# Moving 49 rows between DMA engines: seven of 128 stores written by 14 of the 16 engines

## The chip, the cores and the metric

The kernel runs on one core of one Trainium2 chip. The metric is the device time of the whole program in microseconds; lower is better. A profile comes from one execution; its span, from the first to the last instruction, is about 1.8 us shorter than that execution's time.

## The reference

It is the forward and backward pass of attention with one query per head: 64 heads (2 x 32), 8192 keys, head size 128, bf16.

```python
def _fwd_reference(q, k, v):
    scale = q.shape[-1] ** -0.5
    scores = jnp.einsum("bhqd,bhkd->bhqk", q, k) * scale
    p = _softmax(scores, axis=-1)
    return jnp.einsum("bhqk,bhkd->bhqd", p, v)
# ...
    _out, _vjp = jax.vjp(_f, q, k, v)      # returned: out, dq, dk, dv
    _grads = _vjp(grad_out)
```

For each head, k and v (2 MB each) are read once, and dk and dv (2 MB each) are written once. That is 268 MB in and 268 MB out. The small outputs are out and dq.

## The kernel before

Each 2 MB array of a head lies in SBUF as 128 partitions of one 16 KB row each. A row is 64 consecutive keys. There are 12 such tiles ("slots"). A load fills a slot, the engines compute, the gradient is written over the input in the same slot, and the slot is stored from there. So a new load has to wait for the store of the slot that it takes.

```python
NTILE = 12
# ...
    load_eng = nc.sync        # loads: hardware queue
    store_eng = nc.gpsimd     # stores: GpSimd's software queue
# ...
    def slot_of(i, w):
        n = 2 * i + w
        return n if n < NTILE else slot_of(i - NTILE // 2, 1 - w)

    def load(i, w, pieces=(NCH,)):
        h = heads[i]
        t = kvp.tile([P, NT, D], BF16, tag=f"kv{slot_of(i, w)}", name="kvt")
        h.tile[w] = t
        src = (v_v if w else k_v)[i]
        # ... (one transfer of 128 partitions x 16 KB, except for head 0)
            pin(load_eng.dma_start(out=t[:, n0:n1, :], in_=src[:, n0:n1, :]))
# ...
    qd_nat = evp.tile([P, CH, P], BF16, tag="ev", name="qd_nat")
    for w, a in enumerate((q, grad_out)):
        pin(load_eng.dma_start(out=qd_nat[:BH, w, :], in_=a.rearrange("b h s d -> (b h s) d")))
# ...
    def outer(i, w, c, ends):
        # ... VectorE writes the gradient over h.tile[w] ...
        if c + 1 in ends:
            at = ends.index(c + 1)
            b0, b1 = (ends[at - 1] if at else 0) * CH, (c + 1) * CH
            dst = (dv_v if w else dk_v)[i]
            pin(store_eng.dma_start(out=dst[:, b0:b1, :], in_=h.tile[w][:, b0:b1, :]))
```

For every head but the last, `ends` is one value, so that the store is one transfer of 2 MB. The last head is stored in eight transfers of 512 KB.

Of the kernel before, what the change touches and what calls it, by code (L numbers as in the profile page):

```python
# [16 lines left out]
CW = 64  # L17
NG = 2
NTILE = 12

@with_exitstack
def kernel(
# [12 lines left out]
    B, H, Sq, D = q.shape  # L36
    Sk = k.shape[2]
    P = nc.NUM_PARTITIONS
    assert Sq == 1 and D == P
    BH = B * H  # L40
    assert BH <= P
    NT = Sk // P
# [5 lines left out]
    load_eng = nc.sync  # L48
    store_eng = nc.gpsimd
    pin = tc.keep_in_program_order  # L50
# [25 lines left out]
    def slot_of(i, w):  # L76

        n = 2 * i + w
        return n if n < NTILE else slot_of(i - NTILE // 2, 1 - w)

    def load(i, w, pieces=(NCH,)):
        h = heads[i]
        t = kvp.tile([P, NT, D], BF16, tag=f"kv{slot_of(i, w)}", name="kvt")
        h.tile[w] = t
        src = (v_v if w else k_v)[i]
        c = 0
        for m in pieces:
            n0, n1 = c * CH, (c + m) * CH
            pin(load_eng.dma_start(out=t[:, n0:n1, :], in_=src[:, n0:n1, :]))  # L89
            c += m  # L90

    load(0, 0, (1, 1, 2))

    qd_nat = evp.tile([P, CH, P], BF16, tag="ev", name="qd_nat")
    for w, a in enumerate((q, grad_out)):
        pin(load_eng.dma_start(out=qd_nat[:BH, w, :], in_=a.rearrange("b h s d -> (b h s) d")))  # L96

    load(0, 1)
    for j in range(1, min(NTILE // 2, BH)):
        load(j, 0)  # L100
        load(j, 1)
# [268 lines left out]
    def outer(i, w, c, ends):  # L370

        h = heads[i]
        n0 = c * CH
        shape = [P, CH, D // 2, 2]
        pin(
            nc.vector.tensor_tensor(  # L376
                out=h.tile[w][:, n0 : n0 + CH, :].rearrange("p n (e t) -> p n e t", t=2),
                in0=h.qb[w][:]
                .rearrange("p (e t) -> p e t", t=2)
                .unsqueeze(1)  # L380
                .to_broadcast(shape),
                in1=h.pair[w][:, n0 : n0 + CH, :].unsqueeze(2).to_broadcast(shape),
                op=ALU.mult,
            )
        )
        if c + 1 in ends:
            at = ends.index(c + 1)
            b0, b1 = (ends[at - 1] if at else 0) * CH, (c + 1) * CH
            dst = (dv_v if w else dk_v)[i]
            pin(store_eng.dma_start(out=dst[:, b0:b1, :], in_=h.tile[w][:, b0:b1, :]))  # L390

    A1 = NCH + 4
    O1 = A1 + 1
# [3 lines left out]
    last = list(range(1, NCH + 1))  # L397
    AHEAD = NTILE // 2

    prev = None  # L400
    for g in range(SL * BH + O0 + NCH + 4 - SL):
# [15 lines left out]
        if x := within(O1):  # L417
            outer(x[0], 1, x[1], last if x[0] == BH - 1 else whole)
        if x := within(O0):
            outer(x[0], 0, x[1], last if x[0] == BH - 1 else whole)  # L420
        ev = None
        if g < SL * BH:
            i, r = divmod(g, SL)
# [74 lines left out]
```

## Time and profile before

| kernel before | |
|---|---|
| time, median of 4 runs | 1304.37 us (1304.22 to 1304.51) |
| span of the profiled run | 1303.1 us |
| TensorE busy | 89% |
| DMA | 9 tenths or more busy in 38 of 40 slices, mean 414 GB/s |
| last v load: its 15th completion / its 16th | 1243.0 / 1264.9 us |
| last store: issued / 15th completion / 16th | 1291.6 / 1295.1 / 1301.1 us |

The kernel is limited by DMA. These lines are from the profile page of the kernel before. The line DMA cuts the span into 40 slices and gives the mean busy share of the 16 DMA engines in tenths. The line GB/s gives what they moved in each slice.

```profile
span 1303.1 us, 42566 instructions
...
DMA  9999999999999999999999999999999999999965
GB/s 390 423 427 427 427 427 427 428 426 430 427 427 427 427 427 429 427 428 427 429 427 427 429 427 424 418 420 425 421 416 420 419 421 421 418 421 422 394 281 206
```

What to see is a plateau of 427 GB/s. From the 25th slice on it drops to about 420, and in the last two slices DMA is about half idle. The next lines are from the same page: the queues (packets, MB, share of 16 engines' time) and the transfers (count, size, median us from issue to landing).

```profile
q1 hardware_dynamic: 19040, 268.51, 48.9%
q0 software_dynamic: 19296, 268.44, 48.7%
q8 instruction: 150, 2.46, 0.7%
...
out_dram<-kvt POOLq DMA_DIRECT2D x126, 2048.0 KB, 40.4
kvt<-in_v_dram SPq DMA_DIRECT2D x64, 2048.0 KB, 49.3
kvt<-in_k_dram SPq DMA_DIRECT2D x63, 2048.0 KB, 49.4
```

Loads wait for stores, and TensorE waits only a little for loads. These are two answers on the waits of the kernel before, the load queue's own and TensorE's. The columns are: who waits, for what, total us, times, longest us.

```profile
SPq L89 <- DMA out_dram<-kvt: 1140.6, 116, 24.2
...
PE tp L166 <- DMA kvt<-in_v_dram: 91.1, 54, 2.3
PE tp L166 <- DMA kvt<-in_k_dram: 17.7, 21, 1.3
```

The mean over 16 engines hides the cause. The trace of the kernel before holds 4288 completions for 268 transfers, 16 for each, and a transfer has landed with the last of them. One engine gives one of the 16: after the 15th of the last store only one engine of sixteen still moves data (0.06, below). Here they are for three stores of the kernel before, sorted, in us after the issue:

```text
issued at  616.0: 15.6 15.7 15.7 16.0 16.1 17.9 22.6 27.6 27.9 28.0 28.0 28.2 28.4 28.5 29.3 42.0
issued at 1021.8: 12.7 12.7 13.1 13.8 13.8 14.4 14.8 18.0 19.9 19.9 19.9 19.9 20.2 20.3 20.6 42.0
issued at 1183.6: seven at 12.7 to 13.6, eight at 16.4 to 18.8, one at 41.9
```

One engine is 13, then 21, then 23 us behind the next slowest. All others get ahead of it and then run short of work, because each slot waits for that engine (the load queue waits 1140.6 us for stores, above). The end of the kernel shows this directly. This is the answer that sums stretches of time (us of each engine's busy time and instruction count, granted clock, DMA share, GB/s), kernel before:

```profile
core 0: us, PE busy (x) PEld busy (x) DVE busy (x) ACT busy (x) POOL busy (x), PEclk, DMA share, GB/s
1205.00:1230.00 25.00, 23.16 (x373) 17.09 (x371) 16.79 (x39) 18.24 (x12) 1.06 (x2) 0.88 1.00 422
1252.00:1256.00 4.00, 3.97 (x74) 3.29 (x76) 2.70 (x9) 3.34 (x5) 0.00 (x0) 1.00 0.08 29
1295.50:1300.50 5.00, 0.00 (x0) 0.00 (x0) 0.00 (x0) 0.00 (x0) 0.00 (x0) 0.50 0.06 26
```

A DMA share of 0.06 is one engine of sixteen (1/16 = 0.0625), and 26 GB/s is what this one engine moved. From 1252 to 1256 us one engine is almost alone (0.08), because it still owes its rows of the last loads. From 1295.5 to 1300.5 us it is alone with its rows of the last stores.

The packet records of the trace can be strung into 16 chains, one for each engine, by matching each packet's end with the next one's start. In the kernel before, most 16 KB rows took exactly 611 ns; a few took much longer, so that the mean is 615 to 620 ns in nearly every chain. In one chain it is 636 ns, and there many rows lie on steps of about 9 ns (618, 627, 636, 646 and so on). The chains carry no numbers. The 150 instruction packets fall on eight other chains, 17 to 20 each; five chains have none, and two more have most of the packets of another small instruction queue (31 in all). One of the 150 took about 0.98 us and the packet after it about 1.0 us, so roughly 1.4 us more work for each (an estimate: 0.98 + 1.0 less the 0.611 of a usual row). These chains are a reconstruction from start and end times; the records do not name engines. A second reconstruction gave the same slow chain and the same eight, but it exchanged chains in the last 100 us; so the ends and idle times of single engines rest on one reconstruction.

### The profile page before, as it was taken

How to read it: one execution, taken by the hardware profiler on the slowest of the kernel's cores; microseconds unless marked ns; L12 is line 12 of the kernel's file. 1: busy time of each engine (PE TensorE's matmuls, PEld its weight loads, DVE VectorE, ACT ScalarE, POOL GpSimd, SP SyncE). 2: the span in 40 equal slices, each digit the busy share in tenths (PEclk: the TensorE clock that was granted, in tenths of full speed). 3: DMA queues.
4: the chain of work that ended last, by engine and by line, in shares of the span. 5: the costliest groups of instructions: out<-in, count | busy, mean ns of one | idle time of the engine just before them, and what ended most of it. 6: DMA issues, size and time to landing. Idle time of an engine off the chain costs nothing.

```text
span 1303.1 us, 42566 instructions
## 1 busy us (share of the span) xinstructions
PE 1154.0 (89%) x19268; PEld 873.0 (67%) x19268; DVE 937.5 (72%) x2122; ACT 974.8 (75%) x641; POOL 72.4 (6%) x142
## 2 busy tenths in 40 slices
PE   6999998889898888988989888989898898888984
PEld 5777776667676666666766666667676676666662
DVE  2888887677776777767777677676776767777776
ACT  6888887777787777777778777777777777777771
POOL 0000000000000000000000000000000000000001
PEclk9999999899898999989989999898898989999986
DMA  9999999999999999999999999999999999999965
GB/s 390 423 427 427 427 427 427 428 426 430 427 427 427 427 427 429 427 428 427 429 427 427 429 427 424 418 420 425 421 416 420 419 421 421 418 421 422 394 281 206
DMA packets 38517, 539.67 MB, mean 414 GB/s; under 512 B 4544, under 2 KB 4544, under 8 KB 5824
## 3 DMA queue, kind: packets, MB, share of 16 engines
q1 hardware_dynamic: 19040, 268.51, 48.9%
q0 software_dynamic: 19296, 268.44, 48.7%
q8 instruction: 150, 2.46, 0.7%
q14 instruction: 31, 0.25, 0.0%
HBM read 268.47 MB, written 268.47 MB: 412 GB/s over the span
## 4 chain that ended last, share of the span: by engine, by line
issue 80%; DMA 11%; POOL 4%; DVE 2%; PE 1%; POOLq 0%; SPq 0%; DVEq 0%
DMA kvt<-in_v_dram 8%; POOL out_dram L390 4%; DMA out_dram<-kvt 3%; DVE kvt L376 1%; PE tp L166 1%; POOLq L390 0%; PE acc L321 0%; DVE sel L344 0%; PE dpw L177 0%; SPq L89 0%; SPq L96 0%; DVE sel L338 0%; PE sw L177 0%; PE acc L358 0%; DVE pair L252 0%
## 5 line engine op out<-in xcount | busy, mean ns | idle before, releaser
L168 ACT COPY ev<-tp 128x2048 bf16<-128x2048 bf16 x512 | 954.0, 1865 | 300.3 <-PE tp L166 290.6
L166 PE MATMUL tp<-ident_bf,kvt 128*128 128x128 bf16 x8192 | 573.4, 226 | 108.9 <-DMA kvt<-in_v_dram 91.1
L376 DVE TENSOR_TENSOR kvt<-qb,pair 128x2048 bf16<-128x2048 bf16 x512 | 621.1, 1214 | 0.2
L166 PEld LDWEIGHTS <-kvt 128*128 128x128 bf16 x8192 | 501.4, 102 | 116.2 <-DMA kvt<-in_v_dram 95.8
L177 PEld LDWEIGHTS <-ev 128*128 128x128 bf16 x8192 | 242.8, 96 | 211.2 <-issue 164.4
L321 PE MATMUL acc<-kvt,dS_pad 128*64 128x512 bf16 x1024 | 177.2, 430 | 1.3 <-DVE dqT L361 1.3
L321 PE MATMUL acc<-kvt,E_pad 128*64 128x512 bf16 x1024 | 159.8, 392 | 0.0
L177 PE MATMUL dpw<-qdT,ev 128*128 128x1 bf16 x4096 | 140.9, 164 | 12.0 <-DVE qb L159 10.7
L189 DVE TENSOR_REDUCE mp<-sw 128x1 f32<-128x64 f32 x64 | 14.3, 224 | 186.5 <-PE sw L177 186.5
L344 DVE SCALAR_TENSOR_TENSOR sel<-acc,diag,sel 128x128 f32<-128x128 f32 x384 | 134.6, 351 | 13.6
L177 PE MATMUL sw<-qdT,ev 128*128 128x1 bf16 x4096 | 142.5, 164 | 1.1 <-ACT ev L168 1.1
L390 POOL DMA_DIRECT2D out_dram<-kvt x134 | 71.3, 532 | 1219.2 <-DVE kvt L376 1186.8
L321 PEld LDWEIGHTS <-dS_pad 128*64 128x64 bf16 x1024 | 38.5, 113 | 26.9 <-issue 9.4
L229 DVE CAST E_pad<-E_f 128x64 bf16<-128x64 f32 x64 | 12.5, 195 | 60.6 <-ACT E_f L220 60.6
L321 PEld LDWEIGHTS <-E_pad 128*64 128x64 bf16 x1024 | 36.3, 108 | 21.0 <-issue 0.2
L358 PE MATMUL acc<-ones,sel 128*128 128x1 f32 x256 | 43.3, 239 | 6.2 <-DVE sel L344 6.2
L264 PE MATMUL dpw<-ld,ones 128*128 128x1 f32 x256 | 46.3, 250 | 0.1
L338 DVE TENSOR_SCALAR sel<-acc,diag 128x128 f32<-128x128 f32 x128 | 44.0, 344 | 0.0
L358 PEld LDWEIGHTS acc<-ones,sel 128*128 128x128 f32 x256 | 39.0, 193 | 7.3 <-DVE sel L344 7.3
L235 DVE CUSTOM_DVE_ANT_0 junk<-E_f,dpw 128x64 bf16<-128x64 f32 x64 | 14.1, 220 | 40.2 <-PE dpw L177 40.2
L159 DVE CAST qb<-dpw 128x128 bf16<-128x128 f32 x128 | 35.4, 277 | 6.0 <-PE dpw L150 6.0
L264 PEld LDWEIGHTS dpw<-ld,ones 128*128 128x128 f32 x256 | 38.2, 188 | 0.5 <-DVE ld L235 0.5
(42 smaller groups left out, 303.2 us busy)
## 6 DMA issues: line engine op xcount, KB each, us to landing
out_dram<-kvt POOLq DMA_DIRECT2D x126, 2048.0 KB, 40.4
kvt<-in_v_dram SPq DMA_DIRECT2D x64, 2048.0 KB, 49.3
kvt<-in_k_dram SPq DMA_DIRECT2D x63, 2048.0 KB, 49.4
out_dram<-kvt POOLq DMA_DIRECT2D x8, 512.0 KB, 11.3
kvt<-in_k_dram SPq DMA_DIRECT2D x2, 512.0 KB, 4.5
kvt<-in_k_dram SPq DMA_DIRECT2D x1, 1024.0 KB, 7.1
out_dram<-nat SPq DMA_DIRECT2D x2, 16.0 KB, 5.0
qd_nat<-in_q_dram SPq DMA_DIRECT2D x1, 16.0 KB, 6.8
```

Of the source, the lines that this page charges most:

```text
L159: pin(nc.vector.tensor_copy(out=h.qb[w][:], in_=h.qbp))
L166: pin(nc.tensor.transpose(tp[:, t, :], src[:, c * CH + t, :], ident_bf[:]))
L168: pin(nc.scalar.copy(out=ev[:], in_=tp[:]))
L177: nc.tensor.matmul(dst[:, c * CH + t : c * CH + t + 1], lhsT=ev[:, t, :], rhs=qdT[:, w, i : i + 1], start=True, stop=True,)
L189: pin(nc.vector.reduce_max(out=h.mp[:], in_=h.s, axis=AX.X))
L264: nc.tensor.matmul(out, lhsT=ones[:].to_broadcast([P, P]), rhs=col, start=True, stop=True)
L321: nc.tensor.matmul(h.acc[w][g : g + CW, :], lhsT=wts[:, n0 : n0 + CW], rhs=rows[:, n0 : n0 + QT, :].rearrange("p n d -> p (n d)"), start=( ...
L338: nc.vector.tensor_scalar(out=h.sel[:], in0=block, scalar1=diag[:, 0:1], scalar2=None, op0=ALU.mult)
L344: nc.vector.scalar_tensor_tensor(out=h.sel[:], in0=block, scalar=diag[:, b : b + 1], in1=h.sel[:], op0=ALU.mult, op1=ALU.add,)
L358: nc.tensor.matmul(h.acc[w][:, 0:1], lhsT=h.sel[:], rhs=ones[:], start=True, stop=True)
L376: nc.vector.tensor_tensor(out=h.tile[w][:, n0 : n0 + CH, :].rearrange("p n (e t) -> p n e t", t=2), in0=h.qb[w][:] .rearrange("p (e t) -> ...
L390: pin(store_eng.dma_start(out=dst[:, b0:b1, :], in_=h.tile[w][:, b0:b1, :]))
```

## The change

The intent is to take work from the slow engine. In the kernel before, each of the 16 engines moves 8 of the 128 rows of a transfer: in the packet chains the 16 KB rows of a queue come mostly in runs of eight between two completions. Seven of the dk stores, evenly spaced over the heads, are split into 126 rows and 2 rows. The 126 rows are meant to go on 14 engines (nine rows each) and the 2 rows on the two left out (one row each). An engine left out loses 7 of its 8 rows in each store, 7 x 7 = 49 rows, and every other gains 7. If the slow engine is left out, it is relieved. The argument `max_dma_last_dim` limits one piece to 8 KB.

The author calls the two left out with 6 engines 4 and 5, with 5 engines 3 and 4, with 7 engines 5 and 6, with 8 engines 6 and 7. These numbers are names. They stand on the assumption that the pair is the same in all changed stores of a kernel and moves by one engine with each step of `FIRST`; no record shows an engine's number.

```diff
+FIRST = 6
+SPREAD = range(5, 64, 9)
 ...
+    def by_rows(eng, dst, src, rows):
+
+        p = 0
+        for m in rows:
+            pin(eng.dma_start(out=dst[p : p + m], in_=src[p : p + m], max_dma_last_dim=NT * D))
+            p += m
+
 ...
     for w, a in enumerate((q, grad_out)):
-        pin(load_eng.dma_start(out=qd_nat[:BH, w, :], in_=a.rearrange("b h s d -> (b h s) d")))
+        rows = a.rearrange("b h s d -> (b h s) d")
+        r0 = FIRST if w == 0 else 0
+        if r0:
+            pin(store_eng.inc_swdge_sem([], [], mode="reset_dge_cursor"))
+            pin(
+                store_eng.dma_start(
+                    out=qd_nat[:r0, w, :], in_=rows[:r0], max_dma_last_dim=D
+                )
+            )
+        pin(load_eng.dma_start(out=qd_nat[r0:BH, w, :], in_=rows[r0:BH]))
 ...
-            pin(store_eng.dma_start(out=dst[:, b0:b1, :], in_=h.tile[w][:, b0:b1, :]))
+            if w == 0 and i in SPREAD:
+                by_rows(store_eng, dst, h.tile[w], (P - 2, 2))
+            else:
+                pin(store_eng.dma_start(out=dst[:, b0:b1, :], in_=h.tile[w][:, b0:b1, :]))
```

## The prediction

That engines 4 and 5 would be those left out was the assumption. The last v load at about 1245, 30 us of compute and stores, 2 and 1 come to 1278, and 2 more to 1280 us. The relief of 30 us is 49 rows of 0.607 us (the packet time of 611 ns less an overlap of 4 ns between packets).

> What bounds the kernel now: DMA, and within it one engine. The slices show the 16 DMA engines at 9 tenths or more up to the last two slices, at 417 to 430 GB/s; PE is busy 89%, ACT 75%, DVE 72%. The load queue's waits are 1140.6 us for out_dram<-kvt: a load goes out when a store frees its slot. PE waits 109 us for loads. In the trace a 16 KB row takes 611 ns on nearly every engine; one chain of packets has 618 to 690 ns.
>
> The 16 completions of each transfer, sorted, show the order of the engines without naming them. Late (store issued at 1183.6 us) they come in three groups: seven at 12.7 to 13.6 us, eight at 16.4 to 18.8, one at 41.9. In mid-run, too, eight trail six or seven; the instruction packets (150 of 16 KB) repeat in a pattern of eight, so I take those eight to carry them. The last engine trails the eight by 4 us at 200 us, 13 at 616, 23.4 at 1184: a steady 2%. Its loads take a constant 49 us, so it closes the slot loop and sets the pace; the others keep a backlog. Its last v row lands at 1264.9 us, the others' at 1242.9. From 1295 to 1301 us it drains alone.
>
> What the change does: for seven dk stores, 126 rows go on 14 engines and 2 rows on the other two. [...]No run of before shows this placement or engine numbers. Engines 4 and 5 lose 7 x 7 = 49 rows, 49 x 0.607 = 30 us (an estimate from the packet time less overlap); every other gains 7 rows, 4.3 us. PE, ACT and DVE keep their work; GpSimd gets eight more issues of 0.5 us, off the path.
>
> On the critical path, if the slow engine is 4 or 5: 30 us cover its 23.4 plus 4.3, so all are nearly even and the eight set the pace. Last v load: 1242.9 + 4.3, less stores that now come later, about 1245. Compute and stores after it took 30 us, apart from the 6 us of drain, which goes. 1245 + 30 + 2 + 1 (span to time) is 1278; I add 2 for sixteen engines close together, any of which can be last.
>
> Predicted: 1280 us, range 1275 to 1296. Faster by over 2% 0.35 (the limit is 1278), within 2% 0.63, slower 0.02.
>
> Right if: the gap from 15th to last completion stays below some 5 us instead of growing to 23; the last v load lands near 1245; late GB/s rise to 427 to 430; the single-engine tail shrinks; PE's wait for loads falls by 15 to 20 us.
>
> Wrong if: the slow engine is neither 4 nor 5 (about 1308, gap as before); [...]the slow engine's extra time does not shrink with its rows; or compute, with PE at 89%, cannot follow a head in 19.9 us instead of 20.2.

## More of the kernel before

The experiments went to the chip in three groups, on three chips, each beside runs of the kernel before on the same chip: left67, pieces_only, n14 and map on the first, left34, left56, n5 and halves on the second, cursor_only, n3, n4 and whole_rows on the third.

## The result

| | before | after |
|---|---|---|
| time, median of 4 runs | 1304.37 us (1304.22 to 1304.51) | 1290.06 us (1289.23 to 1292.59) |
| span of the profiled run | 1303.1 us | 1290.8 us |
| last v load: 15th / 16th completion | 1243.0 / 1264.9 us | 1233.5 / 1235.1 us |
| last work of VectorE | 1293.1 us | 1262.3 us |
| last store: issued / 15th / 16th completion | 1291.6 / 1295.1 / 1301.1 us | 1279.0 / 1282.2 / 1288.4 us |

The ratio of the times is 0.9894, with a 95% interval of 0.9876 to 0.9911. Here and below a ratio is the mean time of one kernel's fast runs over that of the other's of the same rounds, so it is not quite the ratio of the medians quoted. The gain is 14.3 us, where 24 were predicted. The execution profiled was the slowest of the four (1292.59 us).

The page of the kernel after, the same lines as before:

```profile
span 1290.8 us, 42577 instructions
...
DMA  9999999999999999999999999999999999999994
GB/s 390 423 427 428 427 427 426 428 427 427 427 427 428 428 426 425 412 429 426 428 426 427 427 426 428 428 426 424 426 427 428 426 421 424 427 429 426 421 383 185
```

The late slices rise from about 420 to about 426, and only the last one is below 9 tenths. There is something new too: single dips, to 412 in the 17th slice and to 421 in the 33rd. The queues and transfers of the kernel after:

```profile
q0 software_dynamic: 20784, 268.45, 49.4%
q1 hardware_dynamic: 19020, 268.51, 48.8%
...
out_dram<-kvt POOLq DMA_DIRECT2D x119, 2048.0 KB, 67.1
kvt<-in_v_dram SPq DMA_DIRECT2D x64, 2048.0 KB, 20.9
kvt<-in_k_dram SPq DMA_DIRECT2D x63, 2048.0 KB, 21.1
out_dram<-kvt POOLq DMA_DIRECT2D x7, 2016.0 KB, 70.6
```

Loads now land in 21 us instead of 49, and stores in 67 instead of 40. The waits, in the order of those shown of before, plus one of GpSimd that before did not have:

```profile
SPq L98 <- DMA out_dram<-kvt: 1140.4, 116, 24.5
...
PE tp L184 <- DMA kvt<-in_v_dram: 75.4, 43, 5.1
PE tp L184 <- DMA kvt<-in_k_dram: 23.7, 31, 2.0
...
POOL out_dram L411 <- DMA out_dram<-kvt: 128.2, 16, 14.1
```

The load queue waits for stores exactly as long as before, although the kernel is faster. TensorE's wait for loads falls by only 10 us (75.4 + 23.7 = 99.1 against 108.8). GpSimd now waits for its own earlier stores, 128 us in 16 waits. The stretches of time at the end of the kernel after:

```profile
core 0: us, PE busy (x) PEld busy (x) DVE busy (x) ACT busy (x) POOL busy (x), PEclk, DMA share, GB/s
1205.00:1230.00 25.00, 21.62 (x379) 16.48 (x380) 17.88 (x43) 18.51 (x13) 1.62 (x3) 1.00 1.01 417
1252.00:1256.00 4.00, 2.24 (x11) 0.87 (x8) 3.89 (x8) 0.00 (x0) 0.53 (x1) 0.50 0.96 400
1272.00:1276.00 4.00, 0.00 (x0) 0.00 (x0) 0.00 (x0) 0.00 (x0) 0.53 (x1) 0.50 0.56 229
1283.00:1288.00 5.00, 0.00 (x0) 0.00 (x0) 0.00 (x0) 0.00 (x0) 0.00 (x0) 0.50 0.06 26
```

The picture is turned round. From 1252 to 1256 us the DMA is full (0.96, where before it was 0.08). From 1272 to 1276 us no compute engine works any more, and 9 of 16 engines' worth of stores is still moving. In the last 5 us again one engine works alone. The timeline of VectorE in the kernel after ends there (start, us, engine, line, operation, tiles, count, idle time before):

```profile
1259.54 1.12 DVE L362 SCALAR_TENSOR_TENSOR sel<-acc,diag,sel 128x128 f32<-128x128 f32 x3
1261.34 0.22 DVE L379 TENSOR_SCALAR dqT<-acc,rls 128x1 bf16<-128x1 f32 x1 [0.68 <-PE acc L376]
1261.97 0.35 DVE L487 COPY nat<-tps 64x128 bf16<-64x128 bf16 x2 [0.41 <-PE tps L485]
```

So the computing ended at 1262.3 us, 27 us after the last load (before, 28). The 26 us after that (to 1288.4) are stores only.

The table below is worked out from the completion times in the trace: the median, over the transfers issued in each 100 us, of the time from issue to the 15th and to the 16th completion (us).

```text
                     issued from:  100    300    500    700    900   1100
before        loads              49/50  45/49  41/49  37/49  33/50  29/49
before        stores             31/34  33/41  30/41  26/41  21/40  18/41
after         loads              42/42  22/22  20/20  18/19  20/20  18/19
after         stores             39/39  61/61  68/68  68/69  66/70  64/69
pieces_only   loads              45/45  26/31  15/21  15/15  18/18  18/18
pieces_only   stores             37/39  49/57  51/67  44/74  34/72  30/71
whole_rows    loads              48/48  39/44  27/42  21/40  17/38  15/36
whole_rows    stores             32/34  38/46  34/50  32/50  32/52  33/55
```

In the kernel before, the gap between 15th and 16th grows to 20 us in loads and 23 in stores. In the kernel after it stays under 1 us up to 800 us, nearly as predicted; then it grows to 6 us in the stores issued from 1026 us on and 6.5 in the last ones (6.3 at the very last). The experiments below show that the engine that trails here is no longer the one of before. (The last four rows belong to experiments below.) Early in the kernel, each changed store moves some of the waiting from the load queue to the store queue, and there it stays.

### The profile page after: what moved, and what is told of

Same layout as the page of the kernel before. It is cut to its first block, busy times and chain, and to the rows that moved or that the text cites. A ratio compares the mean times of both kernels' runs of the same rounds, so it can differ in the third digit from the quotient of the medians.

```text
span 1290.8 us, 42577 instructions
## 1 busy us (share of the span) xinstructions
PE 1126.7 (87%) x19268; PEld 856.4 (66%) x19268; DVE 936.1 (73%) x2122; ACT 975.1 (76%) x641; POOL 79.3 (6%) x150
## 4 chain that ended last, share of the span: by engine, by line
DMA 37%; another core or an unknown queue 27%; PE 20%; DVE 7%; issue 5%; ACT 1%; SPq 1%; POOL 0%; POOLq 0%; ACTq 0%
DMA kvt<-in_v_dram 17%; DMA kvt<-in_k_dram 13%; PE tp L184 9%; DMA out_dram<-kvt 6%; PE acc L339 5%; DVE kvt L394 4%; PE dpw L195 3%; PE sw L195 2%; DVE sel L362 1%; ACT ev L186 1%; SPq L98 1%; PE dpw L282 1%; DMA qd_nat<-in_q_dram 1%; DVE sel L356 0%
## 5 line engine op out<-in xcount | busy, mean ns | idle before, releaser
L184 PE MATMUL tp<-ident_bf,kvt 128*128 128x128 bf16 x8192 | 556.0, 222 | 99.2 <-DMA kvt<-in_v_dram 75.4
L184 PEld LDWEIGHTS <-kvt 128*128 128x128 bf16 x8192 | 486.4, 100 | 106.7 <-DMA kvt<-in_v_dram 79.1
L339 PE MATMUL acc<-kvt,dS_pad 128*64 128x512 bf16 x1024 | 167.3, 409 | 1.6 <-DVE dqT L379 1.6
L411 POOL DMA_DIRECT2D out_dram<-kvt x127 | 68.0, 535 | 1121.0 <-DVE kvt L394 950.5
```

The source lines that it names most:

```text
L184: pin(nc.tensor.transpose(tp[:, t, :], src[:, c * CH + t, :], ident_bf[:]))
L339: nc.tensor.matmul(h.acc[w][g : g + CW, :], lhsT=wts[:, n0 : n0 + CW], rhs=rows[:, n0 : n0 + QT, :].rearrange("p n d -> p (n d)"), start=( ...
```

## The experiments

Letters are names of theories. Theory A is the prediction's: one engine, among 4 and 5, is slow, and the change relieves it. Theory B is the rival that the gain comes from something that has nothing to do with which engines are left out, above all the smaller pieces and the earlier loads that follow from them. Theory C, formed when the gain was found short, is that a store of other than 128 rows disturbs the other transfers. All kernels gave correct results. The edits are against the kernel after. "Slow packets" below are pieces of 8 KB that took over 320 ns instead of the usual 309; they are counted in the packet records.

| run | edit in short | median us (4 runs) | its before | ratio, 95% interval |
|---|---|---|---|---|
| cursor_only | no store changed | 1304.64 (1304.25 to 1304.70) | 1304.39 | 1.0002, 0.9987 to 1.0017 |
| pieces_only | 8 KB pieces, all 16 engines | 1305.61 (1304.61 to 1306.27) | 1304.86 | 1.0004, 0.9988 to 1.0021 |
| left34 | `FIRST` = 5 (engines 3, 4 by name) | 1289.27 (1286.78 to 1295.16) | 1304.59 | 0.9888, 0.9858 to 0.9919 |
| left56 | `FIRST` = 7 (engines 5, 6 by name) | 1313.61 (1312.30 to 1315.39) | 1304.59 | 1.0065, 1.0043 to 1.0087 |
| left67 | `FIRST` = 8 (engines 6, 7 by name) | 1312.66 (1311.96 to 1314.35) | 1304.86 | 1.0061, 1.0046 to 1.0076 |
| n3 | 3 stores | 1295.27 (1295.13 to 1295.61) | 1304.39 | 0.9930, 0.9913 to 0.9947 |
| n4 | 4 stores | 1293.65 (1292.85 to 1293.88) | 1304.39 | 0.9917, 0.9902 to 0.9932 |
| n5 | 5 stores | 1285.34 (1284.72 to 1286.19) | 1304.59 | 0.9852, 0.9835 to 0.9870 |
| n14 | 14 stores | 1305.00 (1298.24 to 1312.75) | 1304.86 | 1.0002, 0.9949 to 1.0055 |
| halves | 14 stores as 64 + 64 rows | 1316.68 (1312.82 to 1320.07) | 1304.59 | 1.0091, 1.0064 to 1.0118 |
| map | 16 stores as 120 + 8 rows | 1340.09 (1335.15 to 1343.95) | 1304.86 | 1.0267, 1.0238 to 1.0296 |
| whole_rows | 7 stores, pieces of 16 KB | 1316.42 (1311.91 to 1318.31) | 1304.39 | 1.0088, 1.0065 to 1.0110 |

### 1. left67: the same change, another pair left out

```diff
-FIRST = 6
+FIRST = 8
```

> The same seven stores[...]. Theory A (one slow engine, 4 or 5, sets the pace of before; the change relieves it): the slow engine now has seven rows more, so about 1304 + 4 = 1308 us, and the gap between 15th and last completion grows to 23 us again. Rival B (the gain comes from the 8 KB pieces and the two-part stores, which move the backlog from the loads to the stores: load landing 49 to 21 us): the same as the change, about 1290 us, whichever engines are left out.

By the author's names engines 6 and 7 are left out here instead of 4 and 5; the passage cut assumed it. Measured: 1312.66 us, 7.8 us slower than before, with the last completion again 25 to 40 us behind the 15th in the stores issued between 700 and 1200 us. The sign follows `FIRST` with the stores and the pieces unchanged, so B falls as the main cause. The loss is bigger than the 4.3 us of seven more rows on the slow engine. That is the first sign of a cost that A doesn't have.

### 2. pieces_only: smaller pieces, no row moved

```diff
-                by_rows(store_eng, dst, h.tile[w], (P - 2, 2))
+                by_rows(store_eng, dst, h.tile[w], (P,))
```

> The same seven stores in 8 KB pieces, but all 128 rows in one transfer over 16 engines, eight rows each: the pieces without the placement. Theory A: no relief, about 1304 us and a gap of 23 us. Rival B: about 1290 us. Both: if it is the smaller pieces that make the stores fall behind the loads[...], the median load landing falls from 49 us towards 20 to 30 us and that of the stores rises from 40 towards 60 to 70 us.

Measured: 1305.61 us, the time of before. Yet its transfers look like those of the kernel after. The page of pieces_only:

```profile
out_dram<-kvt POOLq DMA_DIRECT2D x126, 2048.0 KB, 67.1
kvt<-in_v_dram SPq DMA_DIRECT2D x64, 2048.0 KB, 21.4
kvt<-in_k_dram SPq DMA_DIRECT2D x63, 2048.0 KB, 21.5
```

The last load landed at 1250.2 us, 15 us earlier than before, and the kernel ended at the same time. This shows that the landing time of loads is not the measure. It fits an engine that ends when it has moved its rows, whichever queue it serves first. In the table above, the gap of the slow engine sits entirely in the stores here (30 against 71 us at 1100 us), while it sat in both before. In both traces the two queues started nearly equal numbers of pieces: while the first changed store of the kernel after went out (149 to 159 us), 164 of its 8 KB pieces and 173 load rows of 16 KB were started, and loads had 68% of the bytes; in the kernel before it was 129 rows against 130 in the same stretch. So, with store pieces of half the size, the waiting moves to the stores.

### 3. n14: twice as many stores

```diff
-SPREAD = range(5, 64, 9)
+SPREAD = range(3, 58, 4)
```

> Fourteen stores instead of seven with engines 4 and 5 left out. Theory A: the slow engine is no longer last; every engine with nine rows has seven rows more than in the change, 7 x 0.607 = 4.2 us, and the last of the engines that carry instruction packets ends that much later: 1290 + 4 = 1294 us. If the slow engine still set the pace after the change, it would lose another 30 us of work and the time would fall well below 1290. Rival B: twice the effect, about 1277 us.

Measured: 1305.00 us, 11 us above the expectation, with an unusual scatter: 1298.24, 1299.53, 1310.47 and 1312.75. The profiled run is the fastest of the four; in it the last store landed on twelve engines at 1287 us and on four at 1289 to 1294. Row counts alone do not explain it. The speed of the slices is below that of the kernel after, more often than just where a changed store runs. The page of n14:

```profile
GB/s 389 422 427 427 426 426 428 427 424 425 423 426 428 423 425 416 417 424 418 425 418 419 425 419 420 419 422 424 422 420 418 418 417 424 421 423 418 427 413 220
```

### 4. map: stores of 120 and 8 rows

```diff
-SPREAD = range(5, 64, 9)
+SPREAD = range(2, 63, 4)
...
-                by_rows(store_eng, dst, h.tile[w], (P - 2, 2))
+                by_rows(store_eng, dst, h.tile[w], (P - 8, 8))
```

> A map: sixteen dk stores of 120 rows[...] and 8 rows[...]. Theory A: no engine is relieved for good, so about 1304 us (within 3). What I want from it is the trace: which engine numbers carry instruction packets and which one is slow. Rival B: sixteen stores in 8 KB pieces, at least the gain of seven, 1290 us or less.

Measured: 1340.09 us, 36 us above the expectation. It was meant to leave out one engine after another, each of them once, and so to tie the packet chains to engine numbers. That failed: the records could not be ordered safely, and the placement that the expectation assumed was not shown. What it did show is 494 slow packets of 4096, which together took 162 us longer than normal. As in n14, the surplus came with more stores of other than 128 rows. From here theory C stood beside A.

### 5 and 6. left34 and left56: which of the two engines

```diff
-FIRST = 6
+FIRST = 5     # left34
+FIRST = 7     # left56
```

> [...]Theory A (one slow engine): if it is 4, about 1290 us as in the change; if it is 5, about 1312 us, as the run that left out 6 and 7 (1312.66). A rival to a single slow engine (both 4 and 5 slow, each relieved by the change): between, some 1300 to 1305 us here and in the run that leaves out 5 and 6.

> [...]Theory A: the opposite of the run before, about 1290 us if the slow engine is 5, 1312 us if it is 4; exactly one of the two runs gains.

Measured: 1289.27 us with `FIRST` = 5 and 1313.61 us with 7. With 6 it had been 1290.06, with 8 it had been 1312.66. By the names (3 and 4 for 5, 5 and 6 for 7) both fast pairs contain 4, and neither slow pair does, so the slow engine is called engine 4 from here on. (left34 and left56 ran on one chip, left67 on another; on the third only 6 was tried, with three and four stores, and it gained there too.) The number rests on the assumption that the pair moves by one engine with each step of `FIRST`. The pattern of these four times is the one that a single slow engine would give under it; that fits the assumption and does not prove it.

### 7. n5: fewer stores

```diff
-SPREAD = range(5, 64, 9)
+SPREAD = range(7, 64, 12)
```

> Five stores instead of seven. The slow engine keeps 14 rows more than in the change (8.5 us of work); it had some 10 us to spare there. The other engines have 2 rows less (1.2 us) and two disturbances less. Theory A alone: 1289 us, within 2 of the change. Theory C[...]: 1286 to 1288 us. If time only followed the slow engine's rows: 1290 + 9 = 1299 us.

Theory C's 1286 to 1288 us is 1 to 3 us below theory A's 1289, an allowance for two changed stores fewer. Measured: 1285.34 us, ratio 0.9852. It's the best version, 5 us below the change and 4 below left34, which ran with seven stores on the same chip. It is also below every expectation, closest to that of theory C. The page of n5:

```profile
GB/s 389 422 427 427 427 425 428 428 427 427 428 427 428 427 426 429 428 428 426 428 418 423 427 428 428 427 427 428 425 426 428 428 426 429 429 420 424 428 398 240
```

Its last store was issued at 1272.7 us; the 15th completion came at 1281.0 and the last at 1282.2. In the packet chains, the seven engines that carry instruction packets and took nine-row stores and the slow one all end between 1278 and 1282 us, with 0 to 4 us idle. (The eighth with instruction packets is the other one left out, called 5.) This is the balance that the change aimed at. It also shows what seven stores cost: engine 4 had about 10 us to spare in the kernel after, so that the last 14 of the 49 rows bought nothing, while their weight fell on the others.

### 8. halves: two transfers of 64 rows instead of one of 128

```diff
-SPREAD = range(5, 64, 9)
+SPREAD = range(3, 58, 4)
...
-                by_rows(store_eng, dst, h.tile[w], (P - 2, 2))
+                by_rows(store_eng, dst, h.tile[w], (P // 2, P // 2))
```

> Fourteen stores, each in two transfers of 64 rows[...]. Theory C: packets of twice the usual time appear (8 KB rows of about 606 ns, 16 KB rows of about 1208), a hundred or more, and the time rises above 1304, to some 1310 to 1325. Rival (the extra cost of the changed stores comes from the nine rows alone): 1304 to 1306 us, like the pieces-only run (1305.61), and no more such packets than there (98 slow 8 KB packets in seven stores).

The intent was that every engine keeps 4 + 4 rows of each store, so that no work moves between engines. That is the assumption; no count of rows by engine was taken in this run. Measured: 1316.68 us, 12 us slower than before, and 373 of 3584 pieces were slow, by 159 us in sum over all engines. Compare pieces_only: 98 slow pieces of 1792, 12 us in sum, and no loss of time. The page of halves:

```profile
GB/s 388 424 427 426 428 426 426 428 425 427 424 408 423 405 417 406 393 407 419 402 408 419 401 424 420 419 425 417 422 425 415 424 415 423 418 425 426 425 367 167
```

Between the 12th and the 23rd slice the plateau of 427 breaks down to 393 to 408 again and again. So 14 stores in two transfers of 64 rows cost 12 us, where seven in one transfer of 128 rows, in pieces of the same size, cost none (1305.61 us). If the rows of each engine are the same, as assumed, this is theory C. (Each of these stores is also two transfers instead of one; no run has that alone.) How such stores would slow the others is not shown by any run. The expectation was packets of twice the usual time, and this part missed: of the 373 slow pieces 29 took 580 to 640 ns, and 203 took longer, up to 2313.

The 16 KB rows show the same cost, and its limits. Here is the time above 611 ns of all rows that took over 700 ns, summed over the 16 engines (us):

```text
before 184   cursor_only 183   pieces_only 176
after 109    left34 103        n5 93     n4 114    n3 111
left67 213   left56 231        n14 237   halves 289   whole_rows 355   map 471
```

Every kernel that was slower than its rows account for, apart from n3 and n4, stands in the last line. But left56 and left67 make the same stores as the kernel after and have twice its sum, so the number of rows of a store alone does not decide. And in the kernel after and left34 the sum is lower than before: there theory C does not show.

### 9. cursor_only: the reset and the six rows of q, nothing stored differently

```diff
-SPREAD = range(5, 64, 9)
+SPREAD = ()
```

> No changed store at all: only the reset and the six rows of q on GpSimd, with the other 58 rows on the load queue. All theories: 1304 us, within 2, and load and store landings as in before (49 and 40 us), since every engine has the rows of before.

Measured: 1304.64 us, ratio 1.0002; loads land in 49.3 us and stores in 40.5, as before. The reset call and the load of six rows of q by GpSimd cost nothing that the times show.

### 10 and 11. n3 and n4: the dose

```diff
-SPREAD = range(5, 64, 9)
+SPREAD = range(8, 64, 20)    # n3
+SPREAD = range(8, 64, 15)    # n4
```

> Three stores. Theory A: the slow engine 4 still sets the end and loses 7 rows, 7 x 0.607 = 4.25 us, with each: 1304.4 - 12.7 = 1291.7 us, and the gap between 15th and last completion of the last stores stays at several us.

> Four stores. Theory A: the slow engine sets the end: 1304.4 - 17 = 1287.4 us. With the five-store run at 1285.34 and the change at 1290.06 the best number is then four to six, where the line of the slow engine (-4.25 us per store) meets that of the others (+0.6 us of rows, and something for the disturbance).

Measured: 1295.27 us with three stores (expected 1291.7) and 1293.65 with four (expected 1287.4). Both miss on the slow side. In both, engine 4 was the last to end: in n3 its last completion came 6.4 us after the 15th, in n4 4.4 us. In n3 its chain was busy for 1281.0 us, in n4 for 1281.3, although it had seven rows fewer. Its 16 KB rows took 639.6 ns on average in n4 and 638.5 in n3, and over some two thousand rows each nanosecond is 2 us. That is about half of the 4.5 us that seven rows should have saved; the other half was not found. The second reconstruction gives engine 4 some 637 ns in before and cursor_only and some 638 in n3, n4 and n5 alike. So its rows took longer once stores were changed, by some microseconds in all, and an account in rows can't be better than that; but this does not set n4 apart from n5. The step of 8 us between four and five stores, measured on two chips, is more than seven rows are worth and stays open. The dose curve, taken on three chips whose kernels before agree within 0.5 us, is 1304.6 with no store, 1295.3 with three, 1293.7 with four, 1285.3 with five, 1290.1 with seven and 1305 with fourteen.

### 12. whole_rows: the piece size alone

```diff
-            pin(eng.dma_start(out=dst[p : p + m], in_=src[p : p + m], max_dma_last_dim=NT * D))
+            pin(eng.dma_start(out=dst[p : p + m], in_=src[p : p + m]))
```

> The seven stores of the change with 16 KB rows in one piece instead of two of 8 KB. If the transfer still goes on 14 engines[...]: the relief is as in the change, 1288 to 1291 us, and the loads land later than in the change (the stores no longer fall behind by half). If it is the 8 KB pieces that make the hardware choose 14 engines[...]: no relief, 1304 to 1312 us, and the gap from 15th to last completion is that of before.

Measured: 1316.42 us, slower than before by 12 us. The gap of the slow engine is back (loads 15 against 36 us at 1100 us in the table above), so that engine 4 was not relieved. The packet counts tell of another placement too. Besides the completions the stores left 112 packets of 4 bytes, 16 for each changed store. With 14 engines of nine rows, as in the kernel after, it would be 32, half of the 64 there, since a row is one piece here and not two. 16 would be left by eight rows on each of 15 engines and 6 on the last (two packets for it, and 14 of the second transfer): that is worked out from the count, not seen. The loss is as large as that of halves, and by this count hardly any row moves between engines; that it is the same disturbance is an inference (its long rows sum to 355 us against 289 in halves). The argument `max_dma_last_dim` looks incidental in the diff, but the change depends on it: with pieces of 8 KB the transfer takes 14 engines (1290.06 us), with whole rows the counts say that it does not (1316.42 us).

## Why the prediction was right, and where it was not

**What bounds the kernel: right.** One slow DMA engine set the pace. The sorted completions showed it before; left34, left56 and left67 showed by intervention that it is among those left out with `FIRST` = 5 and 6 and not with 7 and 8 (engine 4 by the names).

**Placement: right, as far as it is shown.** The packets of the changed stores show 14 engines with 18 pieces of 8 KB (nine rows) and two left out. Which two depends on `FIRST`: 1289.3 and 1290.1 us with 5 and 6, 1313.6 and 1312.7 with 7 and 8. The engine numbers were an assumption and stay one. For whole rows the placement did not hold (16 packets of 4 bytes for each changed store, not 32).

**The slow engine's extra time shrinks with its rows: right; its size is less sure.** The gap from the 15th to the last completion stayed under 1 us up to 800 us, and in the chains engine 4 ended with about 10 us to spare. (With three and four stores the gain was 9.1 and 10.7 us, where 12.7 and 17 were expected.) It was no longer the last: that one is an engine with instruction packets and nine-row stores.

**The sum of the end: the step that failed.** The prediction said: "Last v load: 1242.9 + 4.3, less stores that now come later, about 1245. Compute and stores after it took 30 us". The last load landed at 1235.1, not 1245, and the computing then took 27 us as expected, to 1262.3. But the stores went on to 1288.4, 53 us after the last load. The addition holds only while stores keep up with the compute, as they did before the change. After it, the backlog had moved from the load queue to the store queue, and the end was set by the total of each engine's packets. pieces_only shows it separately: the last load came 15 us earlier, and the end did not move. An account by engine would have served better. In the kernel before, the eight engines with instruction packets had finished by 1295.1 us (the 15th completion of the last store) and had stood idle for 16 to 21 us by then, mostly at the end. Without the idle time they would have finished at some 1274 to 1279. Seven rows of 0.611 us make 4.3 more, so 1278 to 1283: an estimate from these numbers. Measured, most of the seven that took nine-row stores ended at 1280 to 1282 us with a few us idle, where the prediction's sum (1245 + 30) put the end at 1275. The agreement is rough, since these engines ended soon after the last store was issued at 1279.0. That 1290 lies in the stated range of 1275 to 1296 is owed to the width of the range: the sum itself was 10 us short.

**The spread of the last engines: mis-sized, and explained only in part.** The prediction added 2 us "for sixteen engines close together". Measured, the last engine, one of those seven, ended at 1288.1, 6 to 7 us after its fellows. Its 16 KB rows took 617.5 ns on average against their 614.9. Why these rows were longer is not shown. Theory C, the disturbance by stores of other than 128 rows, is supported by halves, which lost 12 us though no row was meant to move; left56 and left67 losing 8 to 9 us instead of 4.3 fits it, and so do n14 and map. But in the kernel after itself the slow packets are 64 of 1792, 27 us in sum, and the long rows fewer than before, so that it may have another cause. The two terms together, 5 to 7 us of level and 4 to 5 of spread, cover the 10 us between 1280 and the median of 1290 (the profiled run, from which they are read, took 1292.6).

**TensorE's wait: wrong.** It was to fall by 15 to 20 us and fell by 9.7 (108.8 to 99.1). The late slices' speed rose as predicted in direction: 421 to 429 GB/s from the 25th to the 37th slice, where 416 to 425 had been, against the predicted 427 to 430.

**GpSimd's new wait cost little, as far as the trace shows.** It waited for its own earlier stores 128 us in all; its last stores went out some 4.9 us apart because of it. The engines that limit the end stood idle for only a few us in total (the last one for 0.6). This is an argument from the trace, not an experiment.

**What stays open.** Why engine 4 is slow, and why its slowness varies, is not known. That eight engines are second because of instruction packets is read from the packet chains and wasn't tested by removing such packets. How the disturbing transfers slow the others, and whether they set the spread in the kernel after, is not shown. The misses of n3 and n4 are put down in part to engine 4's own variation because its mean row time moved; why it moved is open.

## What to carry to other kernels

When DMA looks 100% busy, sort the 16 completion times of a late transfer. Here one engine trailed by a growing amount (13, 21 and 23 us) and set the pace, and moving 49 of its rows to others gained 14 us. Size the end by adding up each engine's packets rather than by adding a compute chain to the last load: in pieces_only the backlog moved from loads to stores, the last load came 15 us earlier, and the end stayed. Move only as many rows as bring the slow engine level with the next (five stores here; seven took 4 to 5 us longer, and fourteen gained nothing). Stores cut in another way can cost time by themselves: halves lost 12 us though no row was meant to move.
